# A fused attention and MLP kernel: the prologue's loads issued in turn, batch 0 masked and upsampled by matmul, group 0's first stage run operand by operand and its second stage reordered

## The chip, the cores and the metric

One core of a Trainium2 chip. The metric is the device time of one execution in microseconds (us). The engines are PE (matmul), PEld (weight load of PE), DVE (vector), ACT (scalar), POOL and SP, which here only issues DMA. A profiled execution gives a span a little shorter than the time on the clock of the runs (336.2 us in the profile of the kernel before, whose run counts as 338.2).

## The reference, cut to what matters

```python
def _attn_ref(q, k, v):                       # each [8 batches, 8 heads, 576, 64]
    q_d, k_d, v_d = (means over 4 neighbouring tokens)
    out_up = np.repeat(softmax_attention(q_d, k_d, v_d), 4, axis=2)
    mask = np.abs(pos[:, None] - pos[None, :]) < 4      # a band of 7
    out_local = softmax_attention(q, k, v, masked by mask)
    return out_up + out_local

def _moe_ref(x, w_in, w_out):                 # x [4608, 512], w_in [512, 2048], w_out [2048, 512]
    h = x @ w_in
    g = h * (1.0 / (1.0 + np.exp(-1.702 * h)))
    return g @ w_out
```

The attention's output, as [4608, 512], is the x of the second part.

## The kernel before

The 4608 tokens are cut into 9 groups of 512. Each group has a first stage, 16 blocks of 4 matmuls with w_in (`mm1`, each block followed by a SiLU on ACT), and a second stage, 4 blocks of 16 matmuls with w_out (`mm2`, each block followed by a copy to `osb` on ACT and a store issued by SP). Batch b+1's attention is sprinkled over group b's matmuls at fixed positions. Batch 0's attention has nothing to hide behind: it is the prologue. A position ("step") below 16 is a block of the first stage; step 16 + n comes before matmul n of the second stage, counted from 0.

```python
def warm(n): ...                              # n matmuls on zeros, meant to hold the clock up (see b2_more_warm)
def mask_local(qd):                           # the band, on DVE, after the exp
    for u in range(2):
        ev = es[2 * qd + u][:, :, 0:300]
        nc.vector.tensor_tensor(out=ev, in0=ev, in1=mask, op=ALU.mult)

def mm2(g, gT, steps):
    if g == 0:
        order = [(t0 + u, c * 4 + f) for t0 in (0, 2) for c in range(4)
                 for u in range(2) for f in range(4)]
    else:
        order = [(t, ffc) for t in range(4) for ffc in range(n_ffc)]
    # [...]
    def store(t, ap, c0, n, eng, q):
        # [...]
        osb = moe_sb.tile([128, n], FP32, name="osb", tag=f"osb{n}", bufs=3)
        eng.activation(out=osb, in_=ap, func=AF.Copy, scale=1.0 / GELU_SCALE)
        q.dma_start(out=out[r0 : r0 + 128, c0 : c0 + n], in_=osb)
    for t, ffc in order:
        # [...]
        for f in steps.get(n, ()):  f()       # n counts the matmuls of the second stage
        n += 1
        # [...]
        nc.tensor.matmul(ops[t], lhsT=gT[...], rhs=w_out_bf[:, ffc, :], ...)
        if ffc == n_ffc - 1:
            store(t, ops[t], 0, d_model, nc.scalar, nc.sync)      # SP's queue

POS_0 = [14, 16, 34, 48, 56, 64, 72]          # steps of batch 1's attention in group 0
load_v(0); load_qk(0, 0); ...                 # prologue: v first, on SP's queue
# [...]
for hp in range(4):                           # one head pair of batch 0 after the other
    x[hp] = transp(y[hp])
    merge(0, hp, x[hp], copy_od(x[hp]), eng=nc.gpsimd if hp < 2 else None)
    warm(2)
load_v(1, gate=gate)
for c in range(1, 4):
    load_w_out(c)
def loads_2():                                # batch 2: q, k, then 10 v and 6 v4 loads on SP
    load_qk(2, 0, gate=gate); load_qk(2, 1); load_v(2); load_v4(2)
steps[POS_0[3]].append(loads_2)               # step 48: after 32 matmuls of the second stage
```

The softmax here doesn't subtract the row's maximum and nothing guards it: scores larger than these inputs give would overflow.

## Time and profile before

| | before |
|---|---|
| time, median of 3 runs | 337.58 us (336.59 to 338.2) |
| span in the profile | 336.2 us |
| PE busy, share of the chain of waits | 94%, 84% |
| first matmul of group 0 / gapless from | 29.71 / 31.5 us |
| first matmul of group 1 | 74.3 us |
| PE stands in group 0 | 50.0 to 56.3 us, half clock from 52.4 to 62.6 us |

The busy time of each engine in stretches of 5 us, kernel before (columns: stretch, its length, busy us and instructions of PE, PEld, DVE, ACT, POOL, granted clock of PE, the time that DMA packets took as a share of 16 engines, which can pass 1, GB/s):

```profile
45.00:50.00 5.00, 5.00 (x24) 2.12 (x22) 0.95 (x2) 4.41 (x6) 0.00 (x0) 1.00 1.25 204
50.00:55.00 5.00, 0.01 (x1) 0.04 (x1) 0.00 (x0) 0.08 (x1) 1.06 (x1) 0.74 0.49 80
55.00:60.00 5.00, 3.66 (x119) 2.85 (x119) 0.39 (x1) 1.89 (x3) 1.26 (x1) 0.50 0.02 5
60.00:65.00 5.00, 5.00 (x94) 2.20 (x92) 0.69 (x3) 3.40 (x5) 0.00 (x0) 0.74 0.01 3
65.00:70.00 5.00, 5.00 (x164) 2.65 (x153) 4.86 (x10) 0.00 (x0) 2.16 (x4) 1.00 0.74 200
```

PE is full, then does nothing for 6.3 us, then works at half clock. The view of waits of the same kernel says for what (us in total, times, longest):

```profile
POOL vb_87 L251 <- DMA vf<-in_v_dram: 13.1, 1, 13.1
...
PE vdp L272 <- POOL vb_87 L251: 6.3, 1, 6.3
```

So the chain is a load of batch 1's v, its cast on POOL, and the matmul that needs it. The load was slow while w_out moved beside it: v's five issues between 36 and 46 us took 14.0 us to landing in the median, v's 80 in the whole run 6.6. DMA between 36 and 46 us, kernel before (packets, MB and the time that the packets took, by queue: q0 carries w_out, q1 carries v):

```profile
q0 software_dynamic: 1562, 1.55, 92.0%
q1 hardware_dynamic: 1552, 0.39, 29.6%
```

The packet counts are equal, the bytes four to one (1 KB a packet against 256 B). So in these 10 us v, which is needed first, got a fifth of the bytes.

### The profile page before, as it was taken

Reading aid. Unit: us, or ns where it says so; the run is one execution under the profiler, and the core shown is the slowest. Engines: PE = TensorE matmul, PEld = TensorE weight load, DVE = VectorE, ACT = ScalarE, POOL = GpSimd, SP = SyncE. Lnnn points to the kernel's source line nnn. Section 1 sums busy time; section 2 is a strip of 40 time slices with the busy share of each in tenths; the row PEclk is TensorE's granted clock in tenths of the full one; section 3 lists DMA queues with packets and bytes.
Section 4 is the critical chain, followed back from the end, with each engine's and each line's share of the span. In section 5 each row is a group of like instructions: output and inputs, shape, how many; then the busy total and the mean of one; then the engine's idle time right before and its main releaser. Section 6 shows DMA issues by size and latency. Waiting matters only on the chain.

```text
span 336.2 us, 11213 instructions
## 1 busy us (share of the span) xinstructions
PE 315.9 (94%) x5013; PEld 157.4 (47%) x5013; DVE 135.3 (40%) x217; ACT 184.2 (55%) x315; POOL 138.6 (41%) x164
## 2 busy tenths in 40 slices
PE   6777993999999999999999999999999999999995
PEld 2343442454545455545554545455545554444444
DVE  5766710384067506750675066506750570000000
ACT  2346760546664667466746673668366737424611
POOL 6966802027940892089208920793079000000000
PEclk9699996799999999999999999999999999999999
DMA  8899992199991897199519951898180010011012
GB/s 148 150 159 211 196 200 42 67 181 198 262 190 68 164 204 139 64 181 204 120 67 188 204 114 66 161 208 135 66 163 13 33 67 31 2 63 62 0 55 71
DMA packets 63552, 41.36 MB, mean 123 GB/s; under 512 B 44048, under 2 KB 54416, under 8 KB 63504
## 3 DMA queue, kind: packets, MB, share of 16 engines
q1 hardware_dynamic: 55056, 26.95, 37.5%
q0 software_dynamic: 8304, 13.63, 23.0%
q8 instruction: 39, 0.64, 0.8%
q14 instruction: 9, 0.07, 0.1%
q10 hardware_dynamic: 144, 0.07, 0.1%
HBM read 44.83 MB, written 9.44 MB: 161 GB/s over the span
## 4 chain that ended last, share of the span: by engine, by line
PE 84%; SPq 5%; DMA 4%; POOL 2%; DVE 2%; issue 1%; ACT 1%; POOLq 0%; ACTq 0%
PE ops L558 36%; PE hps L517 33%; SPq L174 5%; DMA qb_128<-in_q_dram 2%; PE sd L315 2%; PE av L354 2%; PE xt L403 2%; PE av L376 2%; DMA vf<-in_v_dram 1%; PE ops L572 1%; PE vdp L272 1%; POOL vb_87 L251 1%; PE warm L465 1%; DVE y L389 1%; PE xt L413 0%
## 5 line engine op out<-in xcount | busy, mean ns | idle before, releaser
L558 PE MATMUL ops<-w_out_bf,gT 128*128 128x512 bf16 x560 | 129.8, 383 | 0.0
L523 ACT ACTIVATE gT<-hps 128x512 bf16<-128x512 f32 x144 | 86.0, 597 | 49.0 <-PE hps L517 49.0
L517 PEld LDWEIGHTS <-w_in_bf 128*128 128x128 bf16 x576 | 55.8, 98 | 68.4 <-issue 2.0
L558 PEld LDWEIGHTS <-gT 128*128 128x128 bf16 x560 | 52.2, 98 | 60.8 <-issue 2.1
L517 PE MATMUL hps<-xT_85,w_in_bf 128*128 128x512 bf16 x144 | 54.6, 379 | 0.8 <-DVE vf L590 0.8
L517 PE MATMUL hps<-xT_82,w_in_bf 128*128 128x512 bf16 x144 | 54.6, 379 | 0.0
L517 PE MATMUL hps<-xT_84,w_in_bf 128*128 128x512 bf16 x144 | 54.6, 379 | 0.0
L517 PE MATMUL hps<-xT_83,w_in_bf 128*128 128x512 bf16 x144 | 54.6, 379 | 0.0
L543 ACT ACTIVATE osb<-ops 128x512 f32<-128x512 f32 (+2 forms) x37 | 22.0, 595 | 40.4 <-PE ops L558 27.2
L340 DVE TENSOR_TENSOR es_90<-es_90,mask 128x600 bf16<-128x600 bf16 x8 | 7.6, 950 | 84.8 <-ACT es_90 L326 84.8
L425 ACT COPY od<-xt 128x384 f32<-128x384 f32 x64 | 21.1, 412 | 36.3 <-PE xt L413 30.8
L389 DVE TENSOR_TENSOR y<-av,rc 128x896 bf16<-128x896 f32 x32 | 34.9, 1092 | 1.1
L545 DVE TENSOR_SCALAR osb<-ops 128x128 f32<-128x128 f32 x1 | 0.3, 291 | 55.3 <-ACT osb L543 55.3
L387 DVE RECIPROCAL rc<-av 128x14 f32<-128x14 f32 x32 | 7.7, 240 | 19.6 <-PE av L376 19.6
L465 PE MATMUL warm<-wz 128*128 128x512 bf16 x41 | 14.1, 476 | 1.2 <-DVE wz L100 1.2
L251 POOL CAST vb_87<-vf 128x2560 bf16<-128x2560 f32 x4 | 9.4, 2344 | 13.1 <-DMA vf<-in_v_dram 13.1
L403 PEld LDWEIGHTS <-y 60*64 60x64 bf16 x640 | 7.4, 107 | 9.2 <-issue 4.3
L403 PE MATMUL xt<-ident,y 60*64 60x57 bf16 (+1 forms) x640 | 9.5, 194 | 1.3 <-issue 0.8
L340 DVE TENSOR_TENSOR es_92<-es_92,mask 128x600 bf16<-128x600 bf16 x8 | 4.2, 529 | 13.8 <-ACT es_92 L326 13.8
L482 ACT ACT_TABLE_LOAD x7 | 9.0, 1283 | 0.1
L478 ACT ACT_TABLE_LOAD x7 | 9.0, 1283 | 0.1
L446 DVE TENSOR_TENSOR xT_84<-xt,od 128x570 bf16<-128x570 f32 x8 | 6.0, 754 | 7.1 <-ACT od L425 7.1
(335 smaller groups left out, 382.5 us busy)
## 6 DMA issues: line engine op xcount, KB each, us to landing
vf<-in_v_dram SPq DMA_DIRECT2D x80, 128.0 KB, 6.6
out_dram<-osb SPq DMA_DIRECT2D x35, 256.0 KB, 2.1
v_96<-in_v_dram SPq DMA_DIRECT2D x36, 192.0 KB, 5.4
w_out_bf<-in_moe_w_out_dram POOLq DMA_DIRECT2D x4, 512.0 KB, 18.0
w_in_bf<-in_moe_w_in_dram POOLq DMA_DIRECT2D x2, 512.0 KB, 6.6
w_in_bf<-in_moe_w_in_dram POOLq DMA_DIRECT2D x1, 1024.0 KB, 11.6
kb_116<-in_k_dram POOLq DMA_DIRECT2D x1, 288.0 KB, 5.3
qb_118<-in_q_dram POOLq DMA_DIRECT2D x1, 288.0 KB, 6.7
```

The source lines that it names most:

```text
L174: nc.sync.dma_start(out=t[64 * par : 64 * par + 64, i], in_=bass.AP(tensor=v.tensor, offset=v[b, 0].offset + (114 * i + KSTART[par]) * D, ...
L251: cp(out=vbs[b % 2][:, i, h, 0:D], in_=vf[b][:, i, h])
L340: nc.vector.tensor_tensor(out=ev, in0=ev, in1=mask, op=ALU.mult)
L389: nc.vector.tensor_tensor(out=y, in0=ov[:, :, :, 0:D], in1=rc.to_broadcast([128, 2, 7, D]), op=ALU.mult,)
L403: nc.tensor.matmul(x[64 * j : 64 * j + 64, par, 57 * i + c0 : 57 * i + c1], lhsT=y[64 * pos : 64 * pos + 60, par, i, :], rhs=ident[64 * po ...
L425: nc.scalar.copy(out=od[:, 4 * t0 : 4 * (t0 + n)].rearrange("p (t f) -> p t f", f=4), in_=x[:, xx, 288 : 288 + n, None].to_broadcast([128, ...
L465: nc.tensor.matmul(t, lhsT=wz[:, 0:128], rhs=wz, start=True, stop=True)
L478: nc.scalar.preload_act_table_set("exp_and_others")
L517: nc.tensor.matmul(hps, lhsT=w_in_bf[:, dmc, ffc * 128 : (ffc + 1) * 128], rhs=xT[dmc][:, tok0 : tok0 + TG], start=(dmc == 0), stop=(dmc = ...
L523: nc.scalar.activation(out=gT[:, ffc, :], in_=hps, func=AF.Silu, scale=GELU_SCALE)
L543: eng.activation(out=osb, in_=ap, func=AF.Copy, scale=1.0 / GELU_SCALE)
L558: nc.tensor.matmul(ops[t], lhsT=gT[:, ffc, t * 128 : (t + 1) * 128], rhs=w_out_bf[:, ffc, :], start=(ffc == 0), stop=(ffc == n_ffc - 1),)
```

## The change

The intent: give v the engines when it is needed. The loads go in the order q/k, v, w_in, q/k of batch 1, half of w_out, v of batch 1, the rest of w_out, q/k of batch 2; four of them (both v, w_in, w_out's second half) are gated, which means that an engine first copies one element of an earlier load into their buffer, and the load waits for that copy. Further: take DVE's mask multiplies and the merges of batch 0 off the vector engines (the mask becomes 16 small matmuls that add -1e6 outside the band, and the repeat by 4 becomes a matmul with a 0/1 matrix, followed by ACT copies); and start group 0's first stage as soon as one of its four operands (one head pair's part of x) is there, six blocks at a time, each in an accumulator of its own (a `pm` or half of a `pa`, 128x512 f32). The second stage of group 0 is reordered so that w_out's second half is needed only from its 33rd matmul on.

```diff
@@ the prologue's order @@
-    load_v(0)
     load_qk(0, 0)
# [... iotas, warm(23), masks ...]
+    load_v(0, gate=after(kf[0, 0][0:1, 0:1], nc.vector))
     prep_1("k", 0, 0)
     prep_1("q", 0, 0)
     pool_qk(0, 0)
-    sp = scores(0, 0)
+    sp = scores(0, 0, barred=True)
     exp_local(0, sp)
     prep_qk(0, 1)
+    nc.gpsimd.tensor_copy(out=w_in_bf[0:1, 0, 0:1], in_=vf[0][0:1, 1, 0, 0:1])
+    load_w_in(0, 512)
     pool_qk(0, 1)
-    load_w_in(0, 512)
# [... load_w_in(512, 512), load_w_in(1024, 1024), load_qk(1, ...), load_w_out(0), load_w_out(1) ...]
@@ operand by operand @@
+    turned(0, None)                      # transpose, add and copy operand 0
+    o[3] = av(0, 3, 0)
+    y[3] = normalise(o[3])
+    turned(1, 1)
+    part((0, 1), 0)                      # first-stage matmuls of blocks 0, 1 with operand 0
+    turned(2, 2)
+    part((0, 1), 1)
+    part((2, 3), 0, 1)
+    turned(3, 0)
+    part((0, 1, 2, 3), 2)
+    part((4, 5), 0, 1, 2)
+    part(range(6), 3)
@@ second stage of group 0 @@
-            order = [(t0 + u, c * 4 + f) for t0 in (0, 2) for c in range(4)
+            order = [(t0 + u, 4 * c + f)
+                     for t0, c in ((0, 0), (0, 1), (2, 0), (2, 1),
+                                   (0, 2), (2, 2), (0, 3), (2, 3))
                      for u in range(2) for f in range(4)]
-            if ffc == n_ffc - 1:
-                store(t, ops[t], 0, d_model, nc.scalar, nc.sync)
+            if ffc == n_ffc - 1 and not (g == 0 and t == 2):
+                for u in (2, 3) if g == 0 and t == 3 else (t,):
+                    store(u, ops[u], 0, d_model, nc.scalar, nc.sync)
@@ positions @@
-    POS_0 = [14, 16, 34, 48, 56, 64, 72]
+    POS_0 = [16, 18, 27, 54, 68, 60, 76]
     def loads_2():
-        load_qk(2, 0, gate=gate)
-        load_qk(2, 1)
-        load_v(2)
+        load_v(2, gate=gate)
         load_v4(2)
-                steps[POS_0[3]].append(loads_2)
+                steps[POS_0[5]].append(loads_2)
# [... load_v(1) and w_out's second half now issued in turn in group 0 ...]
```

## The prediction

Of the clock, the trace before shows this: PE idle from 6.7 to 10.0 us, then half clock from 11.5 to 18.3 us. Its DMA rate from 18 to 50 us is 198 GB/s in the mean, 155 to 220 in stretches of 2 us.

> **What bounds the kernel now.** The chain of waits is 84% PE. From 74.4 us (group 1's first matmul) it is nearly gapless PE work: 33.5 us for a group with attention, 27.6 without. The change leaves that 262 us tail alone. The loss is before (timeline):
> - Group 0's matmuls start at 29.7 us, gapless from 31.5; effectively at 30.9.
> - PE stands from 50.0 to 56.3 us: POOL's cast of batch 1's v waits until 53.9 for DMA. Then the granted clock is 0.5 to 62 us. From 30.9 a group at full rate would end at 64.4, not 74.4: stall plus slow clock cost 10 us.
>
> The stall is a matter of DMA order. From 18 to 50 us the queues move 190 to 220 GB/s. v (256 B packets) and w_out share the engines: from 36 to 46 us w_out gets 0.31 MB per 2 us, v 0.08. [...] v, needed first, loses.
>
> **What the change does.**
> - Loads go in turn: q/k 0, v 0, w_in, q/k 1, half of w_out, v 1, the rest of w_out, q/k 2. Bytes up to w_out's end stay 9.2 MB, 46 us at 200 GB/s. But v 1 should land near 44 instead of 53.7 us, and only the last parts of group 0's second stage need what lands at 47 to 50.
> - Batch 0's mask multiplies (0.7 to 2.1 us each on DVE) become 16 small matmuls. Merging (ACT copies 0.7 to 1.3 us, POOL adds 1.25, DVE 0.75) becomes matmuls plus ACT copies, estimated 1.2 us per operand from the 0.4 us copies. DVE's four normalisations (1.3 us each) then set the pace.
> - First matmuls run as each operand arrives: 24 of 128 are done soon after the last.
> - v 0 is issued later, and w_in's 1 KB packets slow its last part: landing estimated at 15.5 to 18.5 us (before: 15).
>
> **Sum** (estimate from these durations): v 0 cast by 16 to 18.5, first y at 19.5 to 22, first w_in matmul at 23 to 26, 24 matmuls done at 30 to 32.5: effective start 24.6 to 27.3 us, 3.6 to 6.3 earlier. 33.6 us of PE work follow. Stalls left: 3 to 5 us (second attention steps 6 to 8 matmuls apart, 1.3 to 1.7 us, against 2.7 us for two normalisations or merges). Group 1 starts at 61 to 66 us; middle 63.5, a gain of 11, all critical.
>
> **Predicted: 326.5 us, 8 in 10 between 322 and 331.** Faster by over 2%: 0.90; within 2%: 0.09; slower by over 2%: 0.01.
>
> **What would show it.** Group 1's first matmul at 61 to 66 us, the time after it unchanged; no PE gap over 2 us between 30 us and there; clock 1.0 from about 22 us; vb of batch 1 cast by 48 us; w_out landed by 51; DVE idle under 0.5 us between normalisations.
>
> **What would make it wrong.** v 0 starved by w_in past 19 us, with PE idle long enough to be throttled ([...] here 3.3 us of idle gave 0.5 from 11.5 to 18 us). Gated loads opening DMA gaps, so that w_out holds the second stage past 52 us. A larger gain if the late attention steps hide better.

## More of the kernel before

One more view matters, though the prediction did not use it: what SP issues between 60 and 90 us, kernel before (start, duration, how many issues).

```profile
64.15 1.20 SPq L548 DMA_DIRECT2D out_dram<-osb  x2
65.58 13.65 SPq L174 DMA_DIRECT2D vf<-in_v_dram  x10
79.33 3.02 SPq L186 DMA_DIRECT2D v_96<-in_v_dram  x6
82.45 1.30 SPq L548 DMA_DIRECT2D out_dram<-osb  x2
```

Two stores of group 0 leave first, then batch 2's 16 loads, then the other two stores. This is the order of SP's list in the program.

## The result, and the profile after

The changed kernel is slower: 349.05 us (346.66 to 350.21, 4 runs) against 337.08 us (336.21 to 338.2, 4 runs) of the same rounds. The ratio is 1.0345, interval 1.0283 to 1.0408. Ratios here and below are the mean time of one kernel's runs over that of the kernel before in the same rounds, so not quite the ratio of the medians quoted. Executions over 1.5% slower than the fastest of the same kernel are left out of the means.

| in the profile | before | after | predicted |
|---|---|---|---|
| last cast of v 0 ends | 19.5 | 22.6 | 16 to 18.5 |
| 24 first-stage matmuls done | 36.1 | 39.4 | 30 to 32.5 |
| effective start of group 0 | 30.9 | 34.2 | 24.6 to 27.3 |
| first matmul of group 1 | 74.3 | 70.5 | 61 to 66 |
| group 1, first matmul to group 2's | 34.4 | 50.7 | unchanged |
| from there to the end of the span | 227.4 | 227.2 | unchanged |

(The effective start is the end of the first 24 matmuls less 24 times their spacing of 0.216 us, 39.4 - 5.2.) The last three rows add up to the difference of the spans (348.4 - 336.2 = 12.2 us) but for rounding: -3.8 + 16.3 - 0.2. So the whole loss, and more, sits in group 1, which the prediction had left alone; and the prologue, where the gain was to come from, starts group 0 later than before.

The same stretches of the kernel after as above, moved to where its hole is:

```profile
65.00:70.00 5.00, 4.45 (x146) 2.57 (x146) 3.66 (x8) 2.04 (x6) 0.00 (x0) 1.00 0.25 55
70.00:75.00 5.00, 2.56 (x11) 0.97 (x10) 4.93 (x8) 1.10 (x3) 1.95 (x3) 1.00 0.80 178
75.00:80.00 5.00, 0.00 (x0) 0.00 (x0) 1.13 (x2) 0.00 (x0) 4.92 (x7) 0.76 1.06 198
80.00:85.00 5.00, 0.00 (x0) 0.00 (x0) 0.00 (x0) 0.00 (x0) 4.84 (x6) 0.50 1.13 231
85.00:90.00 5.00, 2.04 (x5) 0.69 (x5) 0.00 (x0) 1.71 (x4) 4.84 (x5) 0.50 1.07 282
```

PE stands for 15 us while DMA is full. The stretch of 50 to 55 us, empty before, holds 4.84 us of PE work now: the hole that the change aimed at is gone, and another one, more than twice as long, has opened over 20 us later. The view of waits after:

```profile
ACT osb L657 <- DMA out_dram<-osb: 15.5, 1, 15.5
PE pm L616 <- ACT gT L627: 14.9, 1, 14.9
```

PE waits for ACT's SiLU, and ACT stands in front of a copy to `osb` until a store has landed. What SP issues, kernel after:

```profile
66.34 7.81 SPq L214 DMA_DIRECT2D vf<-in_v_dram  x10
74.20 3.05 SPq L226 DMA_DIRECT2D v<-in_v_dram  x6
77.36 10.43 SPq L662 DMA_DIRECT2D out_dram<-osb  x4
```

And ACT's copies of the four results of group 0, with the SiLU behind them:

```profile
66.13 0.60 ACT L657 ACTIVATE osb<-pm 128x512 f32<-128x512 f32 x1 [1.11 <-PE pm L672]
...
67.92 0.60 ACT L657 ACTIVATE osb<-pm 128x512 f32<-128x512 f32 x1 [1.19 <-PE pm L672]
...
70.71 0.60 ACT L657 ACTIVATE osb<-pa 128x512 f32<-128x512 f32 x1 [0.20 <-PE pa L672]
86.83 0.60 ACT L657 ACTIVATE osb<-pa 128x512 f32<-128x512 f32 x1 [15.52 <-DMA out_dram<-osb]
87.32 1.08 ACT L627 ACTIVATE gT<-pm 128x512 bf16<-128x512 f32 x2
```

Read together: the first result is ready to store at 66.7 us, but SP has just begun batch 2's 16 loads, and issues the first store at 77.36. It lands at 86.7. `osb` has three buffers, so the fourth copy waits for that store; the SiLUs of group 1 stand behind it on ACT, and PE, with both of its accumulators (two `pm`) full after 8 matmuls of group 1, stands too. When PE starts again its clock is 0.5 until 91.3 us. (It had dropped to half at 77.6 us, 4.6 us into the hole; in the kernel before it dropped at 52.4 us, 2.4 us into the hole there.)

In the prologue, two lines of the kernel after show the late v (the last of its casts on DVE) and a wait of PE that no semaphore explains:

```profile
21.96 0.61 DVE L291 CAST vb<-vf 128x512 bf16<-128x512 f32 x1 [3.79 <-DMA vf<-in_v_dram]
...
31.74 0.19 PE L493 MATMUL pa<-up,y 128*64 128x3 bf16 x1 [1.31 <-issue]
```

### The profile page after: what moved, and what is told of

Read it like the earlier page. It is cut to its first block, busy times and chain, and to the rows that moved or that the text cites. A ratio compares the mean times of both kernels' runs of the same rounds, so it can differ in the third digit from the quotient of the medians.

```text
span 348.4 us, 11242 instructions
## 1 busy us (share of the span) xinstructions
PE 313.1 (90%) x4999; PEld 160.2 (46%) x5056; DVE 129.1 (37%) x216; ACT 183.2 (53%) x321; POOL 138.0 (40%) x168
## 4 chain that ended last, share of the span: by engine, by line
PE 83%; SPq 5%; DMA 5%; issue 4%; POOL 1%; DVE 1%; ACT 1%; POOLq 0%; DVEq 0%; ACTq 0%
PE pm L616 34%; PE pm L672 32%; SPq L214 4%; PE pa L351 3%; DMA out_dram<-osb 3%; PE pa L408 2%; DMA vf<-in_v_dram 2%; PE pa L616 2%; PE pa L369 2%; PE pa L430 2%; PE pa L457 2%; PE pa L672 1%; PE pm L687 1%; SPq L226 1%; PE pm L572 0%
## 5 line engine op out<-in xcount | busy, mean ns | idle before, releaser
L616 PE MATMUL pm<-xT,w_in_bf 128*128 128x512 bf16 x528 | 121.7, 383 | 16.1 <-ACT gT L627 14.9
L672 PE MATMUL pm<-w_out_bf,gT 128*128 128x512 bf16 x493 | 114.1, 379 | 5.4 <-issue 5.2
L627 ACT ACTIVATE gT<-pm 128x512 bf16<-128x512 f32 x136 | 80.9, 598 | 45.8 <-PE pm L616 45.8
L616 PEld LDWEIGHTS <-w_in_bf 128*128 128x128 bf16 x576 | 56.0, 98 | 83.6 <-issue 18.3
L657 ACT ACTIVATE osb<-pm 128x512 f32<-128x512 f32 (+2 forms) x35 | 20.7, 593 | 39.9 <-PE pm L672 27.8
L443 DVE TENSOR_TENSOR y<-pa,rc 128x896 bf16<-128x896 f32 x32 | 34.9, 1092 | 1.1
L553 DVE TENSOR_TENSOR xT<-pa,od 128x570 bf16<-128x570 f32 x28 | 21.1, 753 | 10.4 <-ACT od L532 9.6
L380 ACT ACTIVATE es<-pa 128x600 bf16<-128x600 f32 x32 | 19.7, 668 | 8.6 <-PE pa L351 8.3
L297 POOL TENSOR_TENSOR v<-v 112x512 f32<-112x512 f32 x18 | 22.8, 1264 | 0.0
L260 DVE STREAM_TRANSPOSE qT<-qb 128x576 f32<-128x576 f32 x16 | 19.9, 1242 | 1.5 <-DMA qb<-in_q_dram 1.4
L260 DVE STREAM_TRANSPOSE kT<-kb 128x576 f32<-128x576 f32 x16 | 20.0, 1248 | 0.5 <-DMA kb<-in_k_dram 0.4
L276 POOL TENSOR_TENSOR pq<-qT 128x576 f32<-128x576 bf16 x16 | 18.5, 1157 | 0.0
```

The source lines that it names most:

```text
L260: nc.vector.transpose(out=t32.rearrange("p (i c) -> p c i", c=18), in_=store[b, qd].bitcast(FP32).rearrange("p (c d) -> p c d", c=18),)
L276: nc.gpsimd.tensor_tensor(out=t1, in0=sv[:, :, 0:2, :], in1=sv[:, :, 2:4, :], op=ALU.add)
L297: eng.tensor_tensor(out=t1[0:112], in0=x[:, :, 0:2, :], in1=x[:, :, 2:4, :], op=ALU.add)
L380: nc.scalar.activation(out=es[2 * qd + u][:, :, 0:300], in_=sp[u][:, :, 0:300], func=AF.Exp, scale=inv_sqrt_d,)
L443: nc.vector.tensor_tensor(out=y, in0=ov[:, :, :, 0:D], in1=rc.to_broadcast([128, 2, 7, D]), op=ALU.mult,)
L553: eng.tensor_tensor(out=sub(xT[hp], t0 + 3, (57, 2), (114, 5), (1, 57)), in0=sub(x, 3, (509, 2), (57, 5), (1, 57)), in1=sub(od, 3, (57, 2) ...
```

## The experiments

All kernels gave a correct result. The ratio is to the kernel before of the same rounds. The texts of expectation name theories by letters, each said in its text. "First SiLU" is when the first SiLU of group 0 starts, a mark for the start of full-rate work (c1 has the order of before, which runs one block at a time and so reaches it with 4 matmuls done, the others with over 20). These two columns are from the one profiled execution, and executions of one kernel in the same rounds differ by up to 4.6 us, so a few tenths in them mean nothing. The runs of d and e were on another chip than those of a, b and c, so across them compare ratios.

| label | time, us | ratio (95%) | first SiLU | group 1 starts |
|---|---|---|---|---|
| the change | 349.05 | 1.0345 (1.0283 to 1.0408) | 38.45 | 70.5 |
| a1_stores_first | 335.44 | 0.9930 (0.9881 to 0.9979) | - | - |
| a2_four_osb | 334.82 | 0.9924 (0.9881 to 0.9967) | 37.58 | 69.27 |
| a3_stores_on_act | 333.86 | 0.9913 (0.9866 to 0.9959) | 39.97 | 72.3 |
| a4_w_in_after_v | 346.79 | 1.0292 (1.0242 to 1.0342) | 36.14 | 72.98 |
| b1_v0_ungated | 331.49 | 0.9832 (0.9790 to 0.9874) | 35.26 | 66.96 |
| b2_more_warm | 338.30 | 1.0041 (0.9992 to 1.0091) | 40.07 | 74.29 |
| b3_masks_on_dve | 334.28 | 0.9898 (0.9842 to 0.9954) | 38.45 | 70.14 |
| c1_before_load_order | 334.47 | 0.9933 (0.9882 to 0.9985) | 31.21 (other order) | 71.02 |
| d1_no_warm_at_y | 333.70 | 0.9886 (0.9856 to 0.9917) | 37.09 | 68.78 |
| d2_w_in_after_pooling | 331.61 | 0.9819 (0.9800 to 0.9838) | 35.72 | 67.42 |
| d3_both | 332.49 | 0.9855 (0.9816 to 0.9893) | 35.41 | 67.10 |
| d4_dma_quiet | 344.15 | 1.0189 (1.0146 to 1.0231) | 40.03 | over 80 |
| e1_dma_quieter | 345.78 | 1.0220 (1.0144 to 1.0295) | 35.31 | over 80 |
| e2_both_fewer | 333.19 | 0.9844 (0.9798 to 0.9889) | 38.45 | 70.15 |
| e3_d2_fewer | 332.48 | 0.9825 (0.9777 to 0.9872) | 36.68 | 68.37 |

### The hole in group 1: three ways to take away one wait

The theory is that the store waits for its turn in SP's list and ACT waits for the buffer. The rival is that the DMA engines are simply full of batch 2's loads, so that a store is slow wherever it stands. Three kernels undo a different link each.

a1_stores_first issues batch 2's loads after the first two stores instead of ahead of them:

```diff
-                steps[POS_0[5]].append(loads_2)
+                steps.setdefault(72, []).append(loads_2)
```

> The changed kernel, with batch 2's v and v4 loads issued 12 matmuls later, behind the first two of group 0's four stores instead of ahead of all four on the one queue. Theory A (order on the queue: the fourth store buffer is the first one again, its store stood behind 16 loads, ACT waited 15.5 us for it and PE 14.9 us for ACT): the wait of ACT for the store vanishes (under 1 us), group 1's second stage follows without the 15 us gap, time 331 to 335 us. Theory B (the DMA engines are saturated by batch 2's loads, whatever the order; the first store took 9.4 us from issue to landing): the store still lands late and ACT still waits 5 us or more, time 339 to 345.

Four of its five executions took 333.45 to 336.43 us (median 335.44, about half a microsecond past the text's range), a ratio of 0.993. The fifth, which happened to be the profiled one, took 1094.68 us and is left out as slow: its PE was busy all the time, 0.83 us for each first-stage matmul (449.4 us for 544) where a2 needs 0.22 (121.1 us for 544), its trace holds no record of the granted clock, and the fault is not explained. So this run has a time and no trace of a fast execution; that ACT's wait vanished in it is not shown.

a2_four_osb gives the copies a fourth buffer and leaves SP's list as it is:

```diff
-            osb = moe_sb.tile([128, n], FP32, name="osb", tag=f"osb{n}", bufs=3)
+            osb = moe_sb.tile([128, n], FP32, name="osb", tag=f"osb{n}", bufs=4)
```

> The changed kernel with four instead of three buffers for the stored tiles and the queue's order unchanged. Theory A (the wait for the reused buffer): ACT's wait is gone although the stores still go out at 77 us, time 331 to 335 us, equal to the run with the stores first within 1%. Theory B (saturated DMA, something in group 1 needs batch 2's loads): another wait of 5 us or more takes its place in group 1, time over 339.

334.82 us. SP's list is unchanged, the stores still leave only at 76.06 us, and nobody waits for them any more. ACT's last two copies of group 0, kernel a2_four_osb, run back to back (x2):

```profile
69.47 1.09 ACT L657 ACTIVATE osb<-pa 128x512 f32<-128x512 f32 x2 [0.20 <-PE pa L672]
```

a3_stores_on_act issues group 0's stores from ACT's own queue:

```diff
-                    store(u, ops[u], 0, d_model, nc.scalar, nc.sync)
+                    store(u, ops[u], 0, d_model, nc.scalar, nc.sync if g else nc.scalar)
```

> The changed kernel with group 0's four stores issued from ACT's own queue, so that they pass the 16 loads in order but share the same DMA engines with them at the same time. Theory A: store 1 lands within 4 us of its issue, ACT waits under 2 us, time 331 to 336. Theory B (saturated engines, not order): store 1 takes about the 9 us it took in the changed kernel, ACT waits 5 us or more, time 338 to 345.

333.86 us. The view of ACT and its queue, kernel a3_stores_on_act, shows each store issued as soon as its copy is done, and the fourth copy waiting 0.41 us, where it waited 15.52:

```profile
69.69 0.60 ACT L657 ACTIVATE osb<-pm 128x512 f32<-128x512 f32 x1 [1.19 <-PE pm L672]
70.32 0.34 ACTq L662 DMA_DIRECT2D out_dram<-osb  x1
...
73.49 0.60 ACT L657 ACTIVATE osb<-pa 128x512 f32<-128x512 f32 x1 [0.41 <-ACT osb L657]
```

All three links, broken singly, give back about 14 to 15 us (349.05 less 335.44, 334.82 and 333.86, medians of different rounds), with the same bytes to move. The rival, that a store is slow wherever it stands, falls: in a3 the second store, issued at 70.32 us in the midst of batch 2's loads, landed 3.3 us later. The cause is the order of SP's list together with the reuse of `osb`. But full DMA engines had a part in the length: of ACT's 15.5 us in the change, 6.1 passed before the store was issued and 9.4 until it landed, after the last of the 16 loads (84.6 us); in the kernel before, the first store took 2.0 us. All three beat the kernel before by less than 1%, so the rest of the expected gain is still missing.

### The late v of batch 0

a4_w_in_after_v (on the kernel after, with its hole) keeps w_in back until v's last piece has landed, and does the pooling first:

```diff
-    nc.gpsimd.tensor_copy(out=w_in_bf[0:1, 0, 0:1], in_=vf[0][0:1, 1, 0, 0:1])
-    load_w_in(0, 512)
     pool_qk(0, 1)
+    nc.gpsimd.tensor_copy(out=w_in_bf[64:65, 0, 0:1], in_=vf[0][64:65, 4, 0, 0:1])
+    load_w_in(0, 512)
```

> The changed kernel with w_in's first load held until all of batch 0's v has landed (and batch 0's second pooling ahead of it). Theory C (w_in's 1 KB packets starve v 0: its last piece landed at 21.9 us, and this sets the prologue): v 0's last cast ends by 17.5 us instead of 22.6, group 1's first matmul comes at 65 to 67 instead of 70.5 us, the 15 us wait stays, time 343 to 346 us. Rival D (v 0 is slow by itself, its 256 B packets need till 21 us, or the slow clock rules the prologue): the cast ends after 20 us, group 1 starts within 1.5 us of 70.5, time 347 to 350.

v came earlier, its last cast ran at 18.58 to 19.0 us, and the time hardly moved: 346.79, so what was expected of an earlier v did not come. DMA moved nothing from 18 to 20 us, w_out's last load landed at 61.4 us instead of 56.0, and PE waited 3.5 us for it; the first SiLU came 2.3 us earlier and group 1 2.5 us later. What v gained the stream of loads gave back.

b1_v0_ungated (on a2) issues v 0 first, without a gate, and lets w_in start after the pooling of the second k:

```diff
+    load_v(0)
     load_qk(0, 0)
-    load_v(0, gate=after(kf[0, 0][0:1, 0:1], nc.vector))
-    nc.gpsimd.tensor_copy(out=w_in_bf[0:1, 0, 0:1], in_=vf[0][0:1, 1, 0, 0:1])
+    pool_qk(0, 1, "k")
     load_w_in(0, 512)
-    pool_qk(0, 1)
+    pool_qk(0, 1, "q")
```

> Four store buffers (which took the 15 us wait away), and in the prologue v 0 issued at once beside q/k as before the change, and w_in's first load held by nothing but its place on POOL (after the pooling of the second k). Theory E (the prologue lost its gain because v 0 came too late; the DMA should have no idle stretch): v 0's last cast ends by 18 us (22.3 with four buffers), first y by 22 us (25.8), group 1's first matmul at 63.5 to 66.5 us (69.3), time 327 to 331 us. Rival F (the prologue is bound by the half clock and by gaps in PE's instruction supply, v 0 is hidden behind them): the cast comes earlier, but group 1 starts less than 2 us earlier, time 332 to 335.

331.49 us, ratio 0.9832: the last cast ends at 19.8 (a2: 22.3), the first SiLU comes 2.3 us earlier than a2's, and group 1 at 66.96. The cast misses its text by 1.8 us, group 1 and the time by half a microsecond. w_in's first load was issued at nearly the same time (13.69 us, a2: 13.41), so the difference is v's own gate. So v 0's lateness in the change is shown, and cost some 2 to 3 us. All versions below that beat the kernel before by more than 1.1% drop the gate; the change's idea of "in turn" was wrong for v 0.

b3_masks_on_dve (on a2) puts the band back on DVE (`barred=True` out, `mask_local(0)` and `mask_local(1)` back):

> Four store buffers, with batch 0's masks multiplied on DVE again instead of the 16 mask matmuls. Theory E: DVE has 5 us idle before v 0's last piece, so four multiplications cost nothing there: first y within 0.7 us of the run with four buffers alone, time within 1% of it (332 to 337 us); the mask by matmul then bought nothing as long as v 0 lands late. Rival G (the mask matmuls are what shortens the prologue): time longer by 2 us or more, 337 to 340.

334.28 us, the same as a2 within the interval. The mask by matmul buys nothing here, with v 0 late.

### Half clock, or something else?

PE's clock is 0.5 from 23.0 to 29.8 us in the kernel after. b2_more_warm (on a2) keeps PE busier while it waits for v:

```diff
-    warm(10)
+    warm(24)
```

> Four store buffers, v 0 late as in the change, but 24 instead of 10 warming matmuls while PE waits for v 0. Rival F (the half clock from 22 to 29 us costs time): granted clock 1.0 from 20 us on, the part from v 0's last cast to the start of the first-stage matmuls shrinks from 9.2 us by 1.5 to 2.5 us, time 331 to 333. Theory E (v 0's late landing alone): the shrinking is under 1 us, time 333.5 to 336.

Neither text foresaw the result. The clock was 1.0 from 18.5 to 32.1 us, as wanted, then 0.5 again until 35.5, and the kernel got slower, 338.30 us (a2, in other rounds: 334.82). Two waits of PE had grown or appeared, both with no engine to blame, kernel b2_more_warm:

```profile
31.60 0.29 PE L430 MATMUL pa<-vd,ed 48*64 48x65 bf16 x9 [3.89 <-issue]
...
56.86 0.29 PE L369 MATMUL pa<-qdT,kdT 32*64 32x144 bf16 x5 [2.27 <-issue]
```

d1_no_warm_at_y (on b1) tries the order of PE's work instead: the four warm-up matmuls between the head pairs go, and the fourth head pair's matmuls come before the first transposes:

```diff
-    warm(4)
-    turned(0, None)
     o[3] = av(0, 3, 0)
     y[3] = normalise(o[3])
+    turned(0, None)
```

> The run with v 0 ungated, less the four warming matmuls that stand on PE between the third attention product and the first transposes (1.9 us at half clock), and with the fourth product ahead of those transposes. Theory J (PE's own order holds the operands up after y): no idle gap of DVE before the fourth normalisation (1.5 us before), first silu 1.5 to 3 us earlier (before 35.3), group 1 at 64 to 65.5 us, time 328.5 to 330.5. Rival (the w_in data or PE's instruction supply sets the pace there): first silu less than 1 us earlier, time 331 to 332.5.

DVE's four normalisations now follow each other evenly (the last ends at 27.0 us, b1's at 28.8), and the kernel is no faster: 333.70 us, past the ranges of both texts (d2, in the same rounds: 331.61). PE waits 2.90 us at 29.09, again for nothing that the profile names. d2_w_in_after_pooling (on b1) moves w_in's first load behind the whole pooling, and d3_both joins d1 and d2:

```diff
     pool_qk(0, 1, "k")
-    load_w_in(0, 512)
     pool_qk(0, 1, "q")
+    load_w_in(0, 512)
```

> The run with v 0 ungated, with w_in's first load 2 us later, after all of batch 0's pooling. If w_in's packets still starve the last piece of v 0 there: cast of the last piece ends by 17.8 us (19.8), first silu 1 to 2 us earlier, time 329.5 to 331. If the loads behind it (all 2 us later at most) bind the end of group 0: group 1 not earlier than 66.5 us, time 331 to 333.

> Both of these together, the candidate for a version that beats both kernels: group 1 at 62.5 to 65 us, time 327 to 330 us if the two gains add; the better of the two alone (within 1 us) if a common bound (the loads' end) takes over.

Each makes the start of the chain earlier (first y done at 22.0 and 21.5 us, b1's at 23.5), and the first SiLU does not come earlier (35.72, 35.41, 35.26). In between stands the nameless wait, 3.26 and 3.00 us long (b1's: 0.88). d2 is the best ratio, 0.9819, level with b1.

### The nameless wait: PE is out of instructions

In every kernel these waits fall at one of the same places counted in PE's instructions, a matmul and its weight load being two: number 448, 704 or 960 and so on, always 256 apart (to within the few records that some traces lack). The kernel before has it too, 0.77 us at 28.13. The DMA view lists a queue of kind "instruction", whose packets are 16 KB each, 39 in a run (q8); 39 times 256 is 9984, and PE and PEld of the kernel before show 10026 instructions together. The theory from these numbers: a packet is a block of 256 of PE's instructions; when PE passes into a block, the block after it is asked for; that packet moves among the loads; and where the instructions are short PE uses up 256 of them before the packet is there.

d4_dma_quiet (on b2, whose wait was longest) holds q/k of batch 1 and w_out back until the last operand is copied:

```diff
-    for qd in range(NQ):
-        load_qk(1, qd)
-    load_w_out(0)
-    load_w_out(1)
# [... after turned(3, 0) ...]
+    nc.gpsimd.tensor_copy(out=w_out_bf[0:1, 0, 0:1], in_=xT[3][0:1, 0:1])
+    load_w_out(0); load_qk(1, 0); load_qk(1, 1); load_w_out(1)
```

> A test of PE's gaps that no semaphore explains, not a candidate. The run with 24 warming matmuls had one of 3.9 us at 31.6 and one of 2.3 us at 56.9 us; here the loads behind w_in (q/k 1, half of w_out) wait until the last operand of batch 0 is copied, so that the DMA is quiet from about 28 us to then. Theory K (PE's instructions come over the same DMA engines, and their 16 KB fetch stands behind load packets): no such gap over 0.4 us while the DMA is quiet, although PE's instructions are the same. Rival (PE's sequencer itself, or the clock): a gap of 2 us or more stays at the same place in the program. The time gets longer, 339 to 350 us, since the loads come later.

The wait only fell to 2.76 us, the rival's sign. But the loads had not been quiet when the packet was asked for, at 26 us: w_in still moved until about 30 us. e1_dma_quieter holds the second half of w_in back as well:

```diff
-    load_w_in(1024, 1024)
# [... after turned(3, 0) ...]
+    nc.gpsimd.tensor_copy(out=w_in_bf[0:1, 0, 1024:1025], in_=xT[3][0:1, 0:1])
+    load_w_in(1024, 1024)
```

> d4_dma_quiet with w_in's second half held back as well until the last x is copied, so that no bulk load runs from about 24 us until then. A diagnostic; it will be slow because w_in's second half lands late (estimated 340 to 350 us). Theory K (the unexplained PE gap near 31.5 us is PE waiting for its next packet of instructions, which queues behind load packets): the gap at that point of the program (2.76 us in d4_dma_quiet, 3.89 in b2_more_warm) falls under 0.5 us, and the instruction queue's packet before it starts within 1.5 us of its trigger. Rival L (the gap is something in the program's order or in PE itself): a gap of 2 us or more stays at the same instruction.

The same instruction now waits 0.81 us, against 2.76 in d4 and 3.89 in b2; more than the text's 0.5. The first SiLU came at 35.31 us, b2's at 40.07. (The whole takes longer, as foreseen: what was held back is missed later.) PE's line in d4_dma_quiet, then in e1_dma_quieter:

```profile
31.48 0.29 PE L430 MATMUL pa<-vd,ed 48*64 48x65 bf16 x9 [2.76 <-issue]
```

```profile
28.20 0.29 PE L430 MATMUL pa<-vd,ed 48*64 48x65 bf16 x9 [0.81 <-issue]
```

And all that DMA moved from 24 to 26 us in e1_dma_quieter, one packet of instructions:

```profile
DMA packets 1, 0.02 MB, mean 8 GB/s; under 512 B 0, under 2 KB 0, under 8 KB 0
...
q8 instruction: 1, 0.02, 3.1%
```

In d4 the packet of the same place stood among loads (28 to 30 us):

```profile
DMA packets 128, 0.25 MB, mean 123 GB/s; under 512 B 15, under 2 KB 15, under 8 KB 127
...
q0 software_dynamic: 127, 0.23, 61.6%
q8 instruction: 1, 0.02, 3.0%
```

Set side by side from the traces, when PE passed a boundary of blocks (a count of its instructions in the trace), when the next packet moved, and when PE went on at the next boundary (us):

| kernel | PE enters a block | next packet moves | PE goes on | its wait |
|---|---|---|---|---|
| the change | 25.6 | 29.34 to 30.32 | 31.74 | 1.31 |
| b2_more_warm | 24.9 | 29.15 to 30.09 | 31.60 | 3.89 |
| d1_no_warm_at_y | 22.5 | 26.83 to 27.81 | 29.09 | 2.90 |
| d2_w_in_after_pooling | 21.3 | 25.24 to 26.18 | 27.64 | 3.26 |
| d3_both | 20.9 | 24.13 to 25.07 | 26.44 | 3.00 |
| d4_dma_quiet | 26.0 | 29.22 to 30.20 | 31.48 | 2.76 |
| e1_dma_quieter | 24.7 | 25.78 to 26.78 | 28.20 | 0.81 |
| e3_d2_fewer | 19.7 | 23.02 to 23.96 | 25.37 | 2.54 |

That a packet is asked for by PE's entering a block is inferred from this order, which held in all eight. From entering to the packet's start it is 3.2 to 4.3 us where loads run, and 1.1 us with DMA empty; then 1.0 us for the packet; and PE goes on 1.3 to 1.5 us after its end in all eight. That is 3.5 us at the least, and 5.5 to 6.7 us behind loads, for 256 instructions. Why the packet starts so late among loads the traces do not show.

A long wait was paid for twice here. In b2, d2 and d4 the clock record has 0.5 for 3.4 us, beginning within 0.9 us of the wait's end (b2: 32.1 to 35.5 us), and from its end to the first SiLU it is 8.47, 8.08 and 8.55 us; in the change, a2 and b1, whose waits are 0.77 to 1.31 us, the clock is 1.0 there, and it is 6.71 us in each. Kernel b2_more_warm, clock in the column before the last two:

```profile
28.00:32.00 4.00, 0.40 (x13) 0.35 (x15) 0.37 (x2) 0.30 (x2) 0.00 (x0) 1.00 1.11 210
32.00:34.00 2.00, 2.00 (x36) 1.00 (x34) 1.97 (x3) 0.83 (x4) 0.00 (x0) 0.53 1.11 209
```

The last two experiments take 66 PE instructions out of d3 and d2, by dropping `warm(7)` and `warm(10)` and putting the masks back on DVE:

```diff
-    sp = scores(0, 0, barred=True)       # and the same for scores(0, 1)
+    sp = scores(0, 0)
-    warm(7)
     sd = scores_d(0, 0)
     exp_down(0, sd)
+    mask_local(0)                        # and mask_local(1) after exp_local(1, ...)
-    warm(10)
```

> d3_both with 66 fewer PE instructions ahead of the operands: two of the warm-up loops taken out and batch 0's masks on DVE again. Theory K: the packet boundary that cost d3_both 3.00 us at 26.44 us falls 66 instructions later in the program, part of the wait is hidden, and the first silu comes about 1.4 us earlier than d3_both's 35.41 (34.0 to 34.6); ratio to before 0.976 to 0.982, 329.5 to 331 us. Rival L (the warm-up loops are needed for the clock, and the masks belong on PE): half clock longer around 20 to 28 us, first silu at 35.4 or later, ratio 0.985 or above.

> The same 66 PE instructions taken out of d2_w_in_after_pooling, which keeps its four warm-up matmuls at y and its order of turns. Theory K: first silu 1 to 1.5 us earlier than 35.72 (34.2 to 34.8), ratio 0.976 to 0.980. Rival L: no gain or a loss, ratio 0.982 or above, with half clock over 20 to 28 us.

The rival's sign came true: first SiLU at 38.45 and 36.68 us, 3.0 and 1.0 us later than with the warm-ups, and the times no better (333.19, 332.48). Two things happened, both seen in the trace. The clock was 0.5 for longer, in e2 from 11.7 to 35.6 us, in e3 from 11.5 to 21.7 and again from 25.2 to 28.6 (first d2_w_in_after_pooling, then e3_d2_fewer, in stretches of 4 us with the columns as above):

```profile
16.00:20.00 4.00, 3.84 (x77) 2.27 (x69) 2.66 (x7) 2.83 (x4) 4.00 (x6) 1.00 0.65 99
20.00:24.00 4.00, 3.22 (x179) 2.50 (x176) 3.27 (x6) 2.54 (x4) 3.79 (x5) 1.00 1.22 207
24.00:28.00 4.00, 0.74 (x20) 0.60 (x12) 1.80 (x3) 0.56 (x4) 0.94 (x1) 0.97 1.12 213
```

```profile
16.00:20.00 4.00, 2.06 (x34) 1.47 (x34) 3.24 (x9) 0.66 (x2) 4.00 (x7) 0.50 0.88 122
20.00:24.00 4.00, 2.31 (x126) 1.84 (x118) 2.34 (x4) 2.81 (x3) 3.87 (x4) 0.78 1.21 209
24.00:28.00 4.00, 2.30 (x25) 1.10 (x28) 1.58 (x3) 0.00 (x0) 0.36 (x1) 0.64 1.12 211
```

And the fetch was triggered later: without the warm-ups, instruction 448 came after PE's wait for v (19.7 us, d2's 15.8), so the next packet moved at 23.0 instead of 17.3 us, and a wait of 2.54 us appeared at instruction 704. A warm-up matmul is also an instruction that pulls the program forward while PE has nothing better to do: with 17 of them and 16 mask matmuls d2 reached instruction 448 3.9 us before e3. The expected gain from fewer instructions fails; that the waits are waits for instructions stands, since the wait again ended 1.4 us after its packet, at another instruction.

### The load order on its own

c1_before_load_order takes the kernel before, with its compute, and gives it the change's order of loads from w_out on:

```diff
     load_w_out(0)
+    load_w_out(1)
# [...]
-    load_v(1, gate=gate)
-    for c in range(1, 4):
-        load_w_out(c)
# [... in group 0 ...]
             prep_qk(1, 1)
+            load_v(1, gate=lambda t: nc.vector.tensor_copy(out=t, in_=w_out_bf[0:1, 0, 0:1]))
             pool_qk(1, 1)
+            nc.gpsimd.tensor_copy(out=w_out_bf[0:1, 8, 0:1], in_=vf[1][0:1, 3, 0, 0:1])
+            load_w_out(2)
+            load_w_out(3)
```

> The kernel before with nothing but the change's order of loads for batch 1: two quarters of w_out, then v 1, then the other two quarters (compute untouched). Theory H (before's stall of 6 us and its slow clock came from v 1 queueing against w_out): v 1 cast by 50 us, no PE gap over 3 us in group 0, group 1's first matmul at 65 to 69 instead of 74.4 us, time 328 to 332 us. Rival (the bytes bind: holding w_out back moves the wait to w_out's last quarter): group 1 starts at 71 us or later, time 334 to 338.

334.47 us (a fourth execution, 340.04, was slow and is left out), 0.9933; group 1 starts at 71.0 us, 3.3 earlier than before: the rival's text came true. v 1 was cast from 49.59 to 51.9 us, and the wait moved to w_out's second half, kernel c1_before_load_order:

```profile
53.76 1.04 PE L558 MATMUL ops<-w_out_bf,gT 128*128 128x512 bf16 x2 [4.81 <-DMA w_out_bf<-in_moe_w_out_dram]
```

This suggests that the change's load order needs its reordered second stage; with both, and the fourth buffer (a2), group 1 starts at 69.27, but a2 differs in the prologue too. Here moving a load up moved the wait to another one.

## Why the prediction was wrong

**Wrong, and the largest: "The change leaves that 262 us tail alone".** The prediction took everything after group 1's start as fixed and the earlier start as "a gain of 11, all critical". Group 1 took 50.7 us instead of 34.4. The step that failed was to cost what moved without asking what now stands ahead of what in SP's list. The diff had it: batch 2's 16 loads move from after 32 to after 44 matmuls of the second stage, which is later, but the first two results of group 0, complete after 28 and 32 matmuls before, are now complete only after 52 and 56 (the new order interleaves all four). So the stores fell behind the loads, and the fourth copy meets a three-buffer `osb`. a1, a2 and a3 each break one link of it and get about 14 to 15 us back.

**Wrong: v 0 cast by 16 to 18.5 us.** It was 22.6. The prediction knew the risk ("v 0 starved by w_in past 19 us") and sized it at 3.5 us or less. In the kernel after, between 16 and 21 us, w_in's queue moved 0.54 MB and v's 0.27 MB:

```profile
q0 software_dynamic: 541, 0.54, 72.7%
q1 hardware_dynamic: 1071, 0.27, 30.5%
```

The gate delayed v's issue too. b1, without it, had the cast at 19.8 and gained 3.3 us over a2 in the median (334.82 to 331.49), in other rounds.

**Mis-sized: from v's last cast to 24 matmuls done, 14 us (16 to 30, 18.5 to 32.5).** It took 16.8 us (22.6 to 39.4), and the excess lies between the first y and the first w_in matmul: 6.26 us (26.09 to 32.35), where the sum has 3.5 to 4. "DVE's four normalisations then set the pace" was not it: DVE stood 1.47 us before the fourth, and d1 spaced them evenly and was no faster. PE's wait for instructions (1.31 us in the change, 0.77 to 3.89 in the variants) and half clock (0.5 from 23.0 to 29.8 us, where the prediction has 1.0 from about 22) stood in the way. The traces part the two. Less the wait, the 6.26 us are 4.95 in the change, and likewise 4.91 in a2 and 4.76 in b1, all over half of the time at half clock; in b2, d2, d4 and e1, with the clock at 1.0 up to the wait, they are 3.22, 3.28, 3.00 and 2.97. So the half clock cost about 1.8 us here (an estimate from single profiled executions) and the wait 1.31; and in b2, d1, d2 and d3, which sped up what comes ahead of the wait, the wait was longer (2.90 to 3.89 us).

**Right, or near.** No PE gap over 2 us between the start of group 0's matmuls and group 1: the hole of the kernel before is gone. v 1 was cast by 51.15 us (before: 56.3), but not by the 48 predicted. The stalls left in group 0 were about 2.7 us (70.5 less 34.2 and 33.6; predicted 3 to 5). ACT's four copies per operand took 0.83 us from the first start to the last end (their durations add up to 1.18; estimate 1.2). w_out landed at 56.0, not by 51, but was not waited for. Everything after group 1 took 227.2 us, before 227.4.

The arithmetic closes: the effective start was 34.2 instead of 25.95 us (middle of the range), 8.25 us late, of which 5.35 is v's cast (22.6 less 17.25) and 2.9 the chain after it; less about 1.3 us of smaller stalls, this puts group 1 at 70.5 and not 63.5. Then 15 us of hole, and the half clock behind it.

**Left open.** No run changed the clock alone, so the share of the half clock rests on the comparison above. e1's 0.81 us remain with DMA empty; that it is the time of the packet itself (3.5 us for 256 instructions) follows from the table, and no run varied it. And none of the versions reaches the 326.5 us predicted; the best are b1 and d2, 1.7% and 1.8% faster than before.

## What to carry to other kernels

A queue's list is a resource like an engine (here a store that was ready at 66.7 us left at 77.36, behind 16 loads): when a change moves loads or stores, write down the queue's list before and after, and for each buffer the transfer that frees it and what now stands ahead of that transfer. When a load is moved up, ask which load moves down, and gate nothing that the first matmul waits for (without v 0's gate b1 was 3.3 us faster than a2, in other rounds). And where a prologue is made of hundreds of tiny matmuls, look at waits of PE without an engine to blame: count its instructions. Here such waits fell 256 instructions apart, and in all eight kernels of the table they ended 1.3 to 1.5 us after a packet of the instruction queue.
